# A fused FFT filter and Mish layer: the spectral half rewritten, with a second Mish buffer, DMA copies of the filter and a new instruction order

## The chip, the cores and the metric

The kernel runs on one core of a Trainium2 chip. The metric is the device time of one execution in microseconds, as the median of several executions. A profile covers one execution; its span runs from the first to the last instruction and is 1.3 to 2.1 us shorter than the reported time. PE is the matmul engine, PEld its weight loads, DVE, ACT and POOL are the vector, scalar and GpSimd engines, and SP issues most transfers. No execution here had a second die to compare with, so "slow" only marks runs more than 1.5% above the fastest of the same kernel. The experiments ran on two chips, e5 to e8 and e13 to e15 on one, e1 to e4 and e9 to e12 on the other. The kernel before ran in every round, with medians of 169.0 to 169.6 us.

## The reference, cut to what matters

```python
x = A_x                                   # [1, 2048, 512] bf16
g = sigmoid((x * gate_w).sum(-1))
a = irfft2(rfft2(x) * (w_r + 1j * w_i))   # filter in the frequency domain, fp32
h = x @ w1 + b1                           # 512 -> 1792
b = (h * tanh(softplus(h))) @ w2          # Mish, then 1792 -> 512
return g * a + (1 - g) * b
```

The two dense layers need 448 matmuls of 128 x 128 weights by 512 columns. The FFT is done by matmuls with constant matrices, between which data has to change its layout.

Of the kernel before, what the change touches and what calls it, by code (L numbers as in the profile page):

```python
# [8 lines left out]
BF = mybir.dt.bfloat16  # L9
# [7 lines left out]
NCH = 4  # L17

# [8 lines left out]
def _q_of(c, e):  # L27
    return 64 * c + e


def _build_consts():
    cs = {}
    d = np.arange(D, dtype=np.float64)[:, None]
    k = np.arange(256, dtype=np.float64)[None, :]
    ang = 2 * np.pi * d * k / D
    FD = np.zeros((D, 512))
    FD[:, :256] = np.cos(ang)
    FD[:, 256:] = -np.sin(ang)
    FD[:, 256] = (-1.0) ** np.arange(D)
    cs["FD"] = FD.reshape(4, 128, 512).transpose(1, 0, 2)  # L40
    n = np.arange(D, dtype=np.float64)[None, :]
    kk = np.arange(256, dtype=np.float64)[:, None]
    ang2 = 2 * np.pi * kk * n / D
    GD = np.zeros((512, D))
    GD[:256, :] = 2 * np.cos(ang2)
    GD[256:, :] = -2 * np.sin(ang2)
    GD[0, :] = 1.0
    GD[256, :] = (-1.0) ** np.arange(D)
    GD /= (S * D)
    cs["GD"] = GD.reshape(2, 2, 128, D).transpose(2, 1, 0, 3).reshape(128, 4, D)  # L50
    a = np.arange(64, dtype=np.float64)[:, None]
    e = np.arange(64, dtype=np.float64)[None, :]
    qre = np.array([_q_of(0, ee) for ee in range(64)])
    qim = np.array([_q_of(1, ee) for ee in range(64)])
    M1 = np.zeros((128, 32, 128))
    G1 = np.zeros((128, 32, 128))
    for b in range(32):
        th = -2 * np.pi * e * (32 * a + b) / S
        c_, s_ = np.cos(th), np.sin(th)
        M1[0:64, b, qre] = c_  # L60
        M1[64:128, b, qre] = -s_
        M1[0:64, b, qim] = s_
        M1[64:128, b, qim] = c_
        thi = (2 * np.pi * e * (32 * a + b) / S).T
        ci, si = np.cos(thi), np.sin(thi)
        G1[qre, b, 0:64] = ci
        G1[qim, b, 0:64] = -si
        G1[qre, b, 64:128] = si
        G1[qim, b, 64:128] = ci
    cs["M1"] = M1  # L70
    cs["G1"] = G1
    RF = np.zeros((128, 128))
    RI1 = np.zeros((128, 128))
    for b in range(32):
        for dd in range(32):
            ph = -2 * np.pi * b * dd / 32
            fw = [[np.cos(ph), np.sin(ph)], [-np.sin(ph), np.cos(ph)]]
            iv = [[np.cos(ph), -np.sin(ph)], [np.sin(ph), np.cos(ph)]]
            for m2 in range(2):
                for ci_ in range(2):  # L80
                    for co in range(2):
                        RF[4 * b + 2 * ci_ + m2, 4 * dd + 2 * m2 + co] = fw[ci_][co]
                        RI1[4 * dd + 2 * m2 + co, 4 * b + 2 * ci_ + m2] = iv[co][ci_]
    RI2 = RI1[np.arange(128) ^ 1, :]
    P1k = np.zeros((128, 128))
    P0k = np.zeros((128, 128))
    Jm = np.zeros((128, 128))
    for dd in range(32):
        for m2 in range(2):
            for co in range(2):  # L90
                po = 4 * dd + 2 * m2 + co
                P1k[4 * (31 - dd) + 2 * (1 - m2) + co, po] = 1
                if m2 == 1:
                    P0k[4 * (31 - dd) + 2 + co, po] = 1
                else:
                    P0k[4 * ((32 - dd) % 32) + co, po] = 1
                Jm[po ^ 1, po] = 1
    small = np.stack([RF, RI1, RI2, P0k, P1k, Jm], axis=1)
    cs["SMALL"] = small
    cs["SGN"] = np.where(np.arange(128) % 2 == 0, 1.0, -1.0).astype(np.float32).reshape(128, 1)  # L100
    return cs


class _Task:
    __slots__ = ("name", "eng", "dur", "fn", "deps", "lat", "sem", "semval", "idx", "sig",
                 "start", "done", "succ", "bl", "prio", "xfer", "ninst", "opts", "isdma")

    def __init__(self, name, eng, dur, fn, lat=0.0, prio=0.0):
        self.name = name
        self.eng = eng  # L110
        self.dur = dur
        self.fn = fn
        self.deps = []
        self.lat = lat
        self.sem = None
        self.semval = 0
        self.idx = -1
        self.sig = 0
        self.start = 0.0
        self.done = 0.0  # L120
        self.succ = []
        self.bl = 0.0
        self.prio = prio
        self.xfer = 0.0
        self.ninst = 0
        self.opts = None
        self.isdma = False


OPT_BIAS = {"act": 0.0}  # L130
SCH = dict(eps=0.1, sync=0.1)


class _Cnt:
    def __init__(self, e):
        self._e = e
        self.n = 0

    def __getattr__(self, k):
        f = getattr(self._e, k)  # L140

        def w(*a, **kw):
            self.n += 1
            return f(*a, **kw)  # L144

        return w


class _Graph:
    ENGS = ("pe", "act", "dve", "pool", "sp")  # L150

    def __init__(self):
        self.tasks = []
        self.last_w = {}
        self.readers = {}
        self.cur_prio = 0.0
        self.win_first = None
        self.win_last = None

    def add(self, name, eng, dur, fn, reads=(), writes=(), lat=0.0, deps=(), prio=None):  # L160
        if prio is None:
            prio = self.cur_prio
        t = _Task(name, eng, dur, fn, lat, prio)
        dset = []
        seen = set()

        def _add(d):
            if d is not None and d is not t and id(d) not in seen:
                seen.add(id(d))
                dset.append(d)  # L170

        for d in deps:
            _add(d)
        for r in reads:
            _add(self.last_w.get(r))
        for w in writes:
            _add(self.last_w.get(w))
            for rd in self.readers.get(w, ()):
                _add(rd)
        for r in reads:  # L180
            self.readers.setdefault(r, []).append(t)
        for w in writes:
            self.readers[w] = []
            self.last_w[w] = t
        t.deps = dset
        t.idx = len(self.tasks)
        self.tasks.append(t)
        return t

    def add_multi(self, name, opts, reads=(), writes=(), deps=(), prio=None):  # L190
        e0, d0, f0 = opts[0]
        t = self.add(name, e0, min(o[1] for o in opts), f0, reads=reads, writes=writes, deps=deps, prio=prio)
        t.opts = list(opts)
        return t

    def schedule(self):
        tasks = self.tasks
        for t in tasks:
            t.succ = []
            t.start = -1.0  # L200
        for t in tasks:
            for d in t.deps:
                d.succ.append(t)
        for t in reversed(tasks):
            m = 0.0
            for s_ in t.succ:
                if s_.bl > m:
                    m = s_.bl
            t.bl = t.dur + t.lat + m
        nleft = {id(t): len(t.deps) for t in tasks}  # L210
        ready = [t for t in tasks if not t.deps]
        free = {e: 0.0 for e in self.ENGS}
        order = {e: [] for e in self.ENGS}
        nsched = 0
        EPS = SCH['eps']
        SYNC_LAT = SCH['sync']
        dq_free = 0.0
        dq2_free = 0.0
        while nsched < len(tasks):
            best = None  # L220
            best_est = None
            ests = []
            for t in ready:
                if t.opts is None:
                    est = free[t.eng]
                    for d in t.deps:
                        dd = d.done + (0.0 if d.eng == t.eng else SYNC_LAT)
                        if dd > est:
                            est = dd
                else:  # L230
                    bo = None
                    for (oe, od, of) in t.opts:
                        e_ = free[oe]
                        for d in t.deps:
                            dd = d.done + (0.0 if d.eng == oe else SYNC_LAT)
                            if dd > e_:
                                e_ = dd
                        sc = e_ + od + (OPT_BIAS.get(oe, 0.0) if (self.win_first is not None and self.win_first.start >= 0 and self.win_last.start < 0) else 0.0)
                        if bo is None or sc < bo[0] - 1e-9:
                            bo = (sc, e_, oe, od, of)  # L240
                    est = bo[1]
                    t.eng, t.dur, t.fn = bo[2], bo[3], bo[4]
# [717 lines left out]
```

## The kernel before: what the change and the argument touch

Work is a graph of tasks, each with an engine and an estimated duration; a list scheduler at build time turns it into one instruction order for each engine, with semaphore waits between engines. Every instruction is issued from one helper, so the old profile has one line number (L144) for nearly everything, and one reads it by tile names: `xT` is x transposed, `hsreg` the first layer's output, `ureg` the Mish factor, `bs` the output, `scr` DRAM scratch.

```python
# width FFT: 16 matmuls of 64 x 256 for each of 16 row tiles
ins = e.matmul(ps[64*c:64*c+64, bank, 256*bx:256*(bx+1)], xT[:, dt_, t, bx:128:2],
               FD_sb[:, dt_, 256*c:256*(c+1)], start=(dt_ == 0), stop=(dt_ == 3))
...  # second step, DRAM round trip 1, third step, filter, its inverse, DRAM round trip 2
# inverse width FFT: 4 matmuls of 512 columns for each row tile
ins = e.matmul(ps[:, ybank, :], TT[:, ts_, jj, :], GD_sb[:, jj, :], start=(jj == 0), stop=(jj == 3))
...
# Mish of chunk c, two halves of 3584: exp, ln(1 + .), tanh on ACT in one of two buffers,
# then h * tanh(.) on POOL
G.add(f"{nm}_{c}_{hi}", "act", ..., f_act, ...)
G.add(f"mul_{c}_{fh}_{tl}", "pool", ..., f_mul, ...)
```

## Time and profile before

| | before |
|---|---|
| median time | 169.17 us (169.09 to 169.73) |
| span of the profiled run | 167.8 us |
| PE / DVE / ACT / POOL busy | 156.2 / 100.6 / 118.1 / 78.0 us |
| bytes moved | 24.0 MB |

A row of a window gives its borders, its length, then for each engine the busy time and the instruction count, then the granted PE clock, the DMA share and GB/s. A row of a group gives count, busy time, mean ns of one, and the idle time ahead of it with what ended it. The prediction shows the lines and reads them: PE is busy 93% of the span, and no other engine is above 70%.

### The profile page before, as it was taken

The numbers are of one execution on the slowest core, as the hardware profiler recorded it, in microseconds if no ns is written. First come the engines' busy times: TensorE is split into PE (matmuls) and PEld (weight loads), VectorE is DVE, ScalarE is ACT, GpSimd is POOL, SyncE is SP. The second block draws the span as 40 slices with busy tenths as digits, with TensorE's granted clock in tenths as the row PEclk, the third lists the DMA queues.
The fourth block names the chain that finished last, engine by engine and source line by source line (L and its number), as shares of the span: only waits on it lengthen the run. The fifth ranks groups of instructions, "written<-read, shape, count | busy, mean of one in ns | idle before, by whom it ended". The sixth has DMA issues, their size and how long they took to land.

```text
span 167.8 us, 2686 instructions
## 1 busy us (share of the span) xinstructions
PE 156.2 (93%) x1047; PEld 78.2 (47%) x1047; DVE 100.6 (60%) x170; ACT 118.1 (70%) x90; POOL 78.0 (46%) x79
## 2 busy tenths in 40 slices
PE   1798999995999999999999999999999999999990
PEld 0676733372665333444444444443455555544440
DVE  1233601537577885975799798887167885351533
ACT  3145568792998999999988999999999971220000
POOL 1000160059602699524999800099950399910000
PEclk9999999999999999999999999999999999999998
DMA  5999279992405859400030303035901112000101
GB/s 175 304 413 389 84 263 431 391 399 89 125 0 174 293 164 334 168 4 2 0 125 0 125 0 125 4 125 178 321 4 62 62 64 96 33 34 31 62 0 62
DMA packets 13857, 23.99 MB, mean 143 GB/s; under 512 B 852, under 2 KB 10324, under 8 KB 13076
## 3 DMA queue, kind: packets, MB, share of 16 engines
q1 hardware_dynamic: 13076, 17.77, 30.2%
q0 software_dynamic: 768, 6.05, 9.0%
q8 instruction: 8, 0.13, 0.3%
q14 instruction: 5, 0.04, 0.1%
HBM read 17.52 MB, written 6.29 MB: 142 GB/s over the span
## 4 chain that ended last, share of the span: by engine, by line
PE 77%; DMA 15%; DVE 4%; issue 1%; SPq 1%; ACT 0%; ACTq 0%
PE ps L144 77%; DMA scr<-T 12%; DMA hsreg<-in_A_x_dram 3%; DVE bs L144 2%; DVE T L144 1%; DVE xT L144 1%; SPq L144 1%; DVE hsreg L144 0%; ACT T L144 0%; ACTq L878 0%; SPq L878 0%
## 5 line engine op out<-in xcount | busy, mean ns | idle before, releaser
L144 POOL TENSOR_TENSOR hsreg<-hsreg,ureg 128x896 bf16<-128x896 bf16 x32 | 59.3, 1880 | 14.5 <-ACT ureg L144 14.5
L144 PE MATMUL ps<-xT,w_sb 128*128 128x512 bf16 x224 | 53.2, 380 | 0.2 <-DVE hsreg L144 0.2
L144 PE MATMUL ps<-w_sb,hsreg 128*128 128x512 bf16 x224 | 51.9, 379 | 0.0
L144 ACT ACTIVATE ureg<-ureg 128x3584 bf16<-128x3584 bf16 x16 | 51.0, 3189 | 0.2
L144 DVE TENSOR_SCALAR hsreg<-ps,b1f 128x512 bf16<-128x512 f32 x37 | 27.6, 749 | 14.6 <-PE ps L144 13.4
L144 PEld LDWEIGHTS ps<-xT,w_sb 128*128 128x128 bf16 x224 | 19.1, 97 | 29.9 <-DVE hsreg L144 8.2
L144 PEld LDWEIGHTS ps<-w_sb,hsreg 128*128 128x128 bf16 x224 | 21.6, 98 | 24.5
L144 ACT ACTIVATE ureg<-hsreg 128x3584 bf16<-128x3584 bf16 x8 | 25.5, 3188 | 0.6 <-ACT ureg L144 0.3
L144 DVE TENSOR_SCALAR bs<-ps,omg 128x512 bf16<-128x512 f32 x15 | 11.2, 749 | 16.7 <-PE ps L144 16.6
L144 PE MATMUL ps<-fdgd,xT 128*64 128x256 bf16 x256 | 18.6, 294 | 1.1 <-DMA fdgd<-c_fd 1.0
L144 DVE CAST T<-ps 128x512 bf16<-128x512 f32 x19 | 12.9, 687 | 8.2 <-PE ps L144 8.1
L144 PEld LDWEIGHTS ps<-fdgd,xT 128*64 128x64 bf16 x256 | 14.0, 117 | 4.1 <-issue 1.7
L144 PE MATMUL ps<-fdgd,TT 128*128 128x512 bf16 x64 | 15.4, 379 | 0.0
L144 ACT ACTIVATE hsreg<-ps,b1f 128x512 bf16<-128x512 f32 x19 | 13.0, 685 | 3.4 <-PE ps L144 3.2
L144 DVE SCALAR_TENSOR_TENSOR bs<-ps,gcol,bs 128x512 bf16<-128x512 f32 x16 | 12.0, 749 | 4.2 <-PE ps L144 3.6
L144 DVE COPY xT<-ps 128x512 bf16<-128x512 bf16 x13 | 5.3, 422 | 14.2 <-PE ps L144 14.2
L144 ACT ACTIVATE Abuf<-ps 128x512 bf16<-128x512 f32 x8 | 4.8, 597 | 11.4 <-PE ps L144 11.4
L144 ACT ACT_TABLE_LOAD x9 | 11.5, 1283 | 0.9 <-PEq L945 0.8
L144 ACT ACTIVATE T<-ps 128x512 bf16<-128x512 f32 x13 | 7.5, 593 | 5.0 <-DMA scr<-T 2.9
L144 DVE TENSOR_TENSOR bs<-ps,WaT 128x512 bf16<-128x512 f32 x16 | 10.3, 682 | 0.3 <-PE ps L144 0.3
L144 DVE TENSOR_TENSOR bs<-ps,WbT 128x512 bf16<-128x512 f32 x16 | 10.2, 680 | 0.0
L144 DVE CAST TT<-ps 128x256 bf16<-128x256 f32 x22 | 8.0, 436 | 3.0 <-PE ps L144 3.0
(58 smaller groups left out, 90.5 us busy)
## 6 DMA issues: line engine op xcount, KB each, us to landing
WaT<-in_A_w_r_dram POOLq DMA_DIRECT2D x1, 2056.0 KB, 8.1
WbT<-in_A_w_i_dram POOLq DMA_DIRECT2D x1, 2056.0 KB, 14.0
scr<-T SPq DMA_DIRECT2D x8, 256.0 KB, 3.9
Abuf<-scr SPq DMA_DIRECT2D x2, 1024.0 KB, 6.1
scr<-T SPq DMA_DIRECT2D x4, 512.0 KB, 2.6
Abuf<-scr SPq DMA_DIRECT2D x4, 512.0 KB, 5.3
out_dram<-bs SPq DMA_DIRECT2D x8, 256.0 KB, 2.0
w_sb<-in_B_w_dram SPq DMA_DIRECT2D x2, 896.0 KB, 12.3
```

Of the source, the lines that this page charges most:

```text
L144: return f(*a, **kw)
```

## The change

The intent is less PE work, by a finer factoring of the FFT, and a better packed order. The few words that came with it name only the last steps: a second Mish buffer "so that the last two chunks share table loads", a DMA copy of the filter, eviction writes without stride, and a new order found by search. The diff itself replaces nearly the whole file. Its core, cut:

```diff
+# fold x before the FFT, on POOL: u = left + right half, v = left - right
+return e.tensor_tensor(out=xu[:, a:b_, uv, :], in0=x_sb[:, a:b_, 0:256], in1=x_sb[:, a:b_, 256:512],
+                       op=ALU.add if uv == 0 else ALU.subtract)
+# stages p, d, t, it: 64 matmuls of 128 columns each
+ins = e.matmul(o, xu[:, t, uv, e_:256:2], RF, start=True, stop=True)
+ins = e.matmul(bank(b, c // 2)[:, o:o + 128], zu[:, c, t, :], FD[:, c, :], start=True, stop=True)
 ...
+# evictions: PSUM read with a stride, SBUF written in order
+evac(f"ed{t}", lambda t=t: rD[:, 512*t:512*t+1024].rearrange("p (r u) -> p r u", u=2),
+     lambda b=b2: pair(b).rearrange("p (u r) -> p r u", u=2), 1024, ...)
 ...
+if ri == 0 and wdma:      # upper rows of the real filter part
+    dma(f"{nm}n{fh}", dstv[64:128, f0:f0+32, :], dstv[0:64, f0:f0+32, :], 1.6, ...)
+ubuf = [uT[:], uT[:], uT[:], rW[:, 0:7168] if u3 else uT[:]]   # second Mish buffer, chunk 3
 ...
+# rows 8 to 15 of x transposed by DMA, one DRAM round trip, half-swaps of the spectrum by DMA
-order = G.schedule()      # list scheduler at build time
+G.place(ORDER)            # 539 tasks in a searched order, engine and PSUM slot named for each
```

A piece is the edge step. Frequencies 0 and 256 of each row share a column and are filtered apart, by four small matmuls, two ACT copies, three small DVE operations (xp1, xp2, ead), four more matmuls and a DVE copy. The order keeps POOL off the SBUF port by a dependency behind every DVE task marked `lock`; xp2 and ead, which read two SBUF operands, are not marked.

## The prediction

> **What bounds the kernel now.** I read the share of each engine, then the 40 slices, then the chain that ended last, and last the windows, to see whether the chain's long DMA step is real.
>
> ```profile
> PE 156.2 (93%) x1047; PEld 78.2 (47%) x1047; DVE 100.6 (60%) x170; ACT 118.1 (70%) x90; POOL 78.0 (46%) x79
> ...
> PE   1798999995999999999999999999999999999990
> ```
>
> TensorE (PE) is busy 156.2 of 167.8 us and is below 0.9 only in the first slices, one slice near 42 us, and the last. DVE has 67 us to spare, ACT 50.
>
> ```profile
> 21.46 19.98 DMA scr<-T
> ...
> 56.65 105.60 PE ps L144 x533
> 162.24 0.02 issue
> 162.27 0.76 DVE bs L144
> ```
>
> ```profile
> 24.00:32.00 8.00, 8.00 (x37) 2.68 (x34) 2.86 (x4) 6.63 (x6) 0.00 (x0) 1.00 1.02 423
> 32.00:40.00 8.00, 7.93 (x120) 5.02 (x118) 3.56 (x7) 5.65 (x7) 4.61 (x7) 1.00 0.85 323
> 40.00:48.00 8.00, 5.71 (x75) 4.04 (x76) 4.56 (x7) 6.42 (x5) 4.70 (x3) 1.00 0.23 69
> ```
>
> The chain blames 20 us on a write to DRAM scratch, but the windows (span, then PE's busy time first) show PE at 8.00 and 7.93 of 8 us during it: the transfer is hidden, and only the 2.3 us missing in 40:48 cost anything. From 56.65 to 162.25 nothing but matmuls stands on the chain. So the kernel is bound by the amount of PE work, and I count that first.
>
> The unit prices come from the timeline. Seven 512-column matmuls run from 70.91 to the next group at 72.42: 0.216 us each. Transposes of 128 columns come 12 in 0.84 us, about 0.056 each once the last one's latency of 0.24 is off. The forward FFT along the width, pairs of 64-column tiles, takes 1.0 us per row tile (10.64 to 11.64). PE work of the old kernel: dense 448 x 0.216 = 96.6; x transposes 64 x 0.056 = 3.6; width FFT 16; second step 32 x 0.109 = 3.5; third 16 x 0.216 = 3.5; its inverse 32 x 0.216 = 6.9; inverse second step 64 x 0.056 = 3.6; inverse width FFT 64 x 0.216 = 13.8; gate 1.7. Sum 149. The other 19 us are the wait for x and a half-speed clock at first, the gap at 40, and a tail of 5.6 us after the last matmul (162.2 to 167.8: four DVE operations of 0.75 and an output transfer of about 2).
>
> **What the Trainium skill says.** TensorE: Matmul & The Clock Gate, section "Wait — 56ns, not 53.3ns?", gives 215.7 ns and 55.6 ns for 512 and 128 columns at full clock; the trace agrees with both. ScalarE: Activation LUTs, section "What ACT_TABLE_LOAD costs", gives 1283 ns per load, and the trace shows exactly that (fourth row below; the others, with the mean ns of one after the busy us, are the prices I use):
>
> ```profile
> L144 POOL TENSOR_TENSOR hsreg<-hsreg,ureg 128x896 bf16<-128x896 bf16 x32 | 59.3, 1880 | 14.5 <-ACT ureg L144 14.5
> ...
> L144 ACT ACTIVATE ureg<-ureg 128x3584 bf16<-128x3584 bf16 x16 | 51.0, 3189 | 0.2
> ...
> L144 DVE CAST T<-ps 128x512 bf16<-128x512 f32 x19 | 12.9, 687 | 8.2 <-PE ps L144 8.1
> ...
> L144 ACT ACT_TABLE_LOAD x9 | 11.5, 1283 | 0.9 <-PEq L945 0.8
> L144 ACT ACTIVATE T<-ps 128x512 bf16<-128x512 f32 x13 | 7.5, 593 | 5.0 <-DMA scr<-T 2.9
> ```
>
> VectorE: DVE Perf Modes, section "The perf-mode tier table", puts a bf16 SBUF tensor_tensor of 2048 at 1224 ns. No run here shows it yet (the old DVE multiplies nothing that lies wholly in SBUF); with the author's fixed 0.14 us that leaves 0.53 ns an element, so I estimate 0.68 us for 1024 and 0.55 for 768. SBUF — State Buffer, section "Who interferes with whom", says that a DVE operation with two SBUF inputs and a POOL operation that reads SBUF shut each other out. The old trace can't show that; the new kernel runs many such pairs and orders them itself.
>
> **The change part by part.** The few words name its last steps, but the diff rewrites the whole spectral half. What stays: the two dense layers and Mish, and the PE's 96.6 us.
>
> PE, new: 8 of 16 row tiles are transposed on PE, the others by DMA: 32 x 0.056 = 1.8. The four small transform stages (p, d, t, it) have 64 matmuls of 128 columns each: 256 x 0.056 = 14.3. The inverse to the width (id) 64 x 0.109 = 7.0; the last (ip) 16 x 0.216 = 3.5, of which chunk 3 accumulates straight into the dense output. Gate 1.7, edge and gate rows 0.8. Sum 125.7, **23.5 us less than before**. Thirteen warm-up matmuls (some 2.8 us) lie in the wait for x.
>
> DVE, new, read off the list that names each task's engine. A 1024-element eviction from PSUM I estimate at 687 + 512 x 1.04 = 1.22 us. First dense layer 26 x 1.22 = 31.7; transform evictions 31 x 1.22 = 37.8; filter 22 x 0.68 = 15.0; Mish multiply 23, mixed sizes, 14.2; output scaling 13, 9.5; output adds 8 x 0.42 and one of 0.75, 4.1; input copies 4 x 0.42 = 1.7; filter layout 7 x 0.71, 2 x 1.25 and small ones, 8; gate and edge 3. Sum **about 125, up from 101**. The pieces at 0.71 and 1.25 are the author's figures; nothing in the old trace has them.
>
> ACT, new: Mish has the same elements, but exp in four pieces: per chunk 3 x 7168 x 0.833 ns + 8 x 0.2 = 19.5, so 78.1. Table loads: the list still runs exp2, ln2, tanh2, exp3, ln3, tanh3, so **the second buffer does not bring exp2 and exp3 or ln2 and ln3 together**: nine loads again, 11.5. Nine evictions of 1.02, first layer 2.7, output 2.7, final scaling 11 x 0.67, small 3.5. Sum about 115 against 118.
>
> POOL: 10 pre-additions (18), 9 filter moves (18), 9 multiplies (19), the rest 8: about 64, down from 78. One DRAM round trip in place of two; the upper-row copy by DMA takes two DVE operations of 1.25 us off DVE. Stride-free eviction writes change no duration that I can read here, so I give them nothing.
>
> **Sum on the path.** Start: the old 128 KB piece of x landed at 3.0 us, 1 MB in all by 6.9. The new kernel wants 512 KB of x and 512 KB of w1 first, so I put its first dense matmul at 7.0 us. From there PE has 125.7 - 0.9 = 124.8 us: 131.8. Tail: one half-tile scaling of 0.4 and an output transfer of about 2.1: 134.3 without any wait on the way.
>
> The other two engines give nearly the same floor. ACT: the first exp needs four first-layer tiles, each 0.86, and some transform work on PE, and two evictions: about 14 us. From the first exp to the last tanh the list puts 78.1 + 8 x 1.28 + 16.2 of other ACT work = 104.5: last tanh ends at 118.5. Behind the start of that tanh (2.7 long) PE still has 16.9 us listed, so 118.5 - 2.7 + 16.9 + 2.5 = 135. DVE: 125 between 6 and the end: 131 plus 2.1. **Three engines with floors within 2 us of each other** can't all be fed without gaps. I add 4% of 125 = 5 us for waits between them: **139.5 us**.
>
> **Rivals.** (1) PE work alone sets it, as before. For: the old PE lost only 2.3 us in mid-kernel. Against: it had 50 and 67 us of slack on ACT and DVE. That gives 134 to 136. (2) DVE becomes the bound, because two-input operations and POOL block each other, or because the estimated forms are slower than assumed. For: 125 of 139 us, and each 2% of it is 2.5 us. Against: DVE's PSUM reads, over half of its work, have no second SBUF input. That gives 143 to 148. (3) The DRAM round trip starves PE: 256-byte rows written, then read into rows freed only when filter moves are done. For: the old trace lost 2.3 us behind the same thing at 512-byte rows. Against: between the last write and its first user the list puts 13.6 us of PE work, which a write of 3.9 and a read of 6.1 us (the old medians) fit into. It would cost 2 to 4 us: 141 to 144. (4) Nothing gained, since ACT sets the end. Against: the ACT chain, counted whole, ends at 118. I see no way to 166.
>
> **Range and chances.** The floor is 134, and my sum would have to be 15% off to reach 160. Eight times in ten: 134.5 to 147. Faster by over 2%: 0.97; within 2%: 0.02; slower: 0.01.
>
> **What would show each step.** PE work: matmul count 448 of 512 columns, and far fewer of the rest; about 23 us less busy time. DVE: at 85% or more of the span. ACT: nine table loads, exp and ln alternating by chunk. Waits: PE windows of the middle 2 to 5% below full, its wait behind DVE evictions rather than DMA; if a gap of several us stands before the t stage with a scratch transfer named, rival 3 is right. Start: first dense matmul at 7 us. Tail: 2.5 us behind the last matmul. The prediction is wrong if the early loads or the DMA transposes are late, if DVE's SBUF forms are slower than estimated, or if the waits between three full engines cost 10 us rather than 5.

## The result, and the profile after

The changed kernel took 145.27 us (144.63 to 145.88, four runs), against 169.13 for the kernel before; six more runs later gave 145.32 (143.21 to 145.92), of which the three at 145.9 count as slow, since one run was at 143.21. The ratio of the fast runs was 0.8715 (0.862 to 0.8809) at first and 0.8575 (0.8498 to 0.8651) in the repeat. Ratios are the mean time of one kernel's fast runs over that of the other's of the same rounds, so not quite the ratio of the medians, which is 0.859 at first. The gain is 24 us of 169, where 29.7 were predicted.

The page of the kernel after, with the busy shares and the slices of PE and of the PE clock:

```profile
PE 132.6 (93%) x921; PEld 73.2 (51%) x921; DVE 119.4 (84%) x154; ACT 112.8 (79%) x77; POOL 63.3 (44%) x50
...
PE   4789999889969999999999999997799999999992
...
PEclk9969999999999999999999999999999999999999
```

PE's busy time fell by 23.6 us, from 156.2 to 132.6; the work count of the prediction said 23.5. That they agree to 0.1 is partly luck: the 132.6 holds 2.9 us of warm-up that the count leaves out, and in both kernels PE was busy some 7 us longer than counted (156.2 against 149, 132.6 against 125.7). DVE rose to 119 (125 predicted), ACT is at 113 (115) and POOL at 63 (64). So the engine loads are nearly right, and the miss must lie mostly in starts, clock, gaps and ends. The slices show three dips: the PE clock at 0.6 in the third slice, PE at 6 near 40 us, and PE at 7 near 98.

The chain that ended last, in order of time (start, length, what), shows two of them:

```profile
0.80 4.62 DMA rA<-in_A_x_dram
...
7.70 3.35 PE ps L897 x8
...
12.14 4.32 PE ps L897 x20
...
96.43 0.14 PE ps L801
...
96.60 0.28 ACT tmp L809
...
96.90 0.28 ACT tmp L810
...
97.24 1.19 issue
98.43 0.16 DVE ezb L745
98.59 0.20 DVE tmp L811
...
98.82 1.91 DVE tmp L813
```

The first eight dense matmuls take 3.35 us, 0.42 each; the twenty at 12.14 take 0.216 each. So the array ran at half clock there. Two windows show when:

```profile
4.56:7.98 3.42, 1.86 (x19) 1.07 (x19) 0.85 (x2) 1.19 (x2) 2.33 (x3) 1.00 1.02 353
7.98:11.39 3.41, 3.41 (x12) 1.28 (x10) 0.00 (x0) 0.00 (x0) 3.24 (x2) 0.50 1.09 382
```

The transposes of x just before had run at full speed (8 in 0.62 us from 5.47). So here the clock had been released and was lost again, after 3.4 us in which PE was busy 1.86 us and never idle for longer than 0.74 at a time. And from 96.4 to 102.9 the chain leaves PE for the edge step. The timeline there (start, length, engine, line, operation):

```profile
96.24 6.11 POOL L933 TENSOR_TENSOR rD<-rD,uT 128x1024 bf16<-128x1024 bf16 x3 [3.14 <-ACT uT L921]
...
97.20 1.30 DVE L812 TENSOR_TENSOR tmp<-tmp,wsi 128x128 f32<-128x128 f32 x1 [0.87 <-ACT tmp L810]
...
98.82 1.91 DVE L813 TENSOR_TENSOR tmp<-tmp 128x128 bf16<-128x128 f32 x1
...
100.78 0.20 PE L820 MATMUL ps<-tmp,rD 128*128 128x1 bf16 x2 [1.63 <-DVE tmp L813]
...
102.55 3.85 ACT L918 ACTIVATE rW<-hs 128x2048 bf16<-128x2048 bf16 x2 [2.01 <-DVE hs L904]
```

xp2 (L812) and ead (L813) work on 128 elements a partition, yet take 1.30 and 1.91 us, while POOL multiplies from 96.24 to 102.35. PE loses 1.63 us behind ead. ACT loses 2.01 behind an eviction that stands after them on DVE.

The rows that answer to the prices of before, from the groups by form:

```profile
L514 DVE CAST rD<-ps 128x1024 bf16<-128x1024 f32 x7 | 8.4, 1214 | 0.0
...
L776 DVE TENSOR_TENSOR rC<-rC,rW 128x1024 bf16<-128x1024 bf16 x8 | 5.5, 687 | 0.2 <-DMA tmp<-rC 0.2
...
L920 ACT ACT_TABLE_LOAD x4 | 5.1, 1283 | 0.1
```

The estimates of 1.22 us for an eviction and 0.68 for a filter multiply hold. Table loads are four here, three on L921 and one each on L517 and L743, nine as before.

### The profile page after: what moved, and what is told of

Read it like the earlier page. It is cut to its first block, busy times and chain, and to the rows that moved or that the text cites. A ratio compares the mean times of both kernels' runs of the same rounds, so it can differ in the third digit from the quotient of the medians.

```text
span 142.7 us, 2358 instructions
## 1 busy us (share of the span) xinstructions
PE 132.6 (93%) x921; PEld 73.2 (51%) x921; DVE 119.4 (84%) x154; ACT 112.8 (79%) x77; POOL 63.3 (44%) x50
## 4 chain that ended last, share of the span: by engine, by line
PE 78%; ACT 11%; DVE 4%; DMA 3%; issue 2%
PE ps L949 33%; PE ps L897 27%; PE ps L876 5%; ACT uT L920 4%; DMA rA<-in_A_x_dram 3%; PE ps L837 3%; PE ps L762 3%; ACT uT L921 3%; PE ps L975 2%; PE ps L637 2%; PE ps L603 2%; PE ps L649 1%; DVE tmp L813 1%; ACT L921 1%; ACT L920 1%
## 5 line engine op out<-in xcount | busy, mean ns | idle before, releaser
L897 PE MATMUL ps<-rX,w_sb 128*128 128x512 bf16 x224 | 53.0, 387 | 0.9 <-DVE rX L514 0.5
L949 PE MATMUL ps<-w_sb,hs 128*128 128x512 bf16 (+1 forms) x182 | 40.0, 363 | 0.0
L897 PEld LDWEIGHTS ps<-rX,w_sb 128*128 128x128 bf16 x224 | 21.4, 99 | 26.0 <-issue 1.6
L949 PEld LDWEIGHTS ps<-w_sb,hs 128*128 128x128 bf16 x182 | 17.5, 98 | 17.4 <-DVE hs L933 0.3
L904 DVE TENSOR_TENSOR hs<-ps,b1f 128x1024 bf16<-128x1024 f32 x19 | 23.2, 1227 | 0.9 <-PE ps L897 0.6
L920 ACT ACTIVATE uT<-uT 128x4096 bf16<-128x4096 bf16 (+1 forms) x6 | 19.1, 3190 | 0.1
L921 ACT ACTIVATE uT<-uT 128x4096 bf16<-128x4096 bf16 (+1 forms) x6 | 19.1, 3186 | 0.1
L618 POOL TENSOR_TENSOR rB<-rA 128x1024 bf16<-128x1024 bf16 (+1 forms) x10 | 17.3, 1735 | 4.1 <-DMA rA<-in_A_x_dram 3.2
L918 ACT ACTIVATE uT<-hs 128x2048 bf16<-128x2048 bf16 (+1 forms) x8 | 13.6, 1694 | 5.5 <-DVE hs L904 5.3
L933 POOL TENSOR_TENSOR rD<-rD,uT 128x1024 bf16<-128x1024 bf16 (+1 forms) x7 | 13.4, 1918 | 6.8 <-DVE rD L933 3.2
L949 PE MATMUL ps<-w_sb,rD 128*128 128x512 bf16 x56 | 13.2, 379 | 0.0
L517 ACT ACTIVATE rC<-ps 128x1024 bf16<-128x1024 f32 x8 | 8.0, 1018 | 0.2
```

The costliest lines, as they stand in the source:

```text
L517: return e.activation(o(), i(), AF.Copy)
L618: return e.tensor_tensor(out=xu[:, a:b_, uv, :], in0=x_sb[:, a:b_, 0:256], in1=x_sb[:, a:b_, 256:512], op=ALU.add if uv == 0 else ALU.subt ...
L897: ins = e.matmul(bank(b, i), w1_sb[:, dt_, 128 * ft:128 * (ft + 1)], xT[:, c, dt_, :, :], start=(dt_ == 0), stop=(dt_ == 3))
L904: return e.tensor_tensor(out=hs[hb][:, ft:ft + 2, :], in0=pair(b).rearrange("p (f s) -> p f s", f=2), in1=b1f[:, ft:ft + 2].unsqueeze(2).t ...
L918: return e.activation(o, hsf[hb][:, 512 * a:512 * b_], fn_)
L920: return e.activation(o, o, fn_, bias=1.0)
```

## The experiments

**Theory:** PE's work is still the bound, and the miss is a cold start of the PE clock, the edge step behind POOL, and the difference of span and reported time (how far that held is said below, in the section on the prediction). **Rivals:** DVE, now loaded for 84% of the span, is the bound; or the ACT chain of Mish is. Each kernel below differs from the changed kernel, or from the one named as base, only as shown, and gives the reference's result unless said otherwise.

**e1: more warm-up matmuls.** The warm-up's memset goes first on POOL, and there are 20 matmuls, so that PE is busy until x lands.

```diff
-ones cRF x0 ident warm0 w1_0 ...
+warm0 cRF x0 ones ident w1_0 ...
-NWARM = 13
+NWARM = 20
```

> The first eight dense matmuls took 0.42 us each (half clock) because the 13 warm-up matmuls ended at 4.7 us and x came at 5.4. Here the warm-up starts 0.6 us earlier and has 20 matmuls, so PE is busy until x lands. Theory (PE work and its order set the start of the chain): those eight matmuls take 0.22 us each, first exp starts 1.6 us earlier, total 1.0 to 1.8 us shorter. Rival (the middle is bound by DVE or ACT, which absorb it): clock full, but total within 0.4 us.

Measured: 143.15 us (142.76 to 143.53), 2.1 less. The timeline of PE:

```profile
1.17 3.92 PE L537 MATMUL ps<-hs 128*128 128x256 bf16 x20 [1.17 <-POOL hs L526]
...
7.74 1.90 PE L897 MATMUL ps<-rX,w_sb 128*128 128x512 bf16 x8 [0.52 <-DVE rX L514]
```

The same eight matmuls need 1.90 us in place of 3.35, from the same start, and the first exp of chunk 3 begins at 101.37 in place of 102.55. The spread shrank too. The Trainium skill (TensorE: Matmul & The Clock Gate, section "What's actually happening") says that about 3.4 us of sustained work release the clock, in a window that runs free of the kernel; the old warm-up of 13 lasted 2.9 us. The runs agree in part. With 13, the profiled runs of e2 and e3 below reached the dense matmuls at full clock, that of e9 ran even its transposes at half speed (16 in 2.33 us), and the one above had the clock and lost it. So a short warm-up can fail in two ways; e1, which makes it both longer and nearly gapless up to x, does not tell them apart. The ten runs of the changed kernel lie at 143.2 us (one), 144.6 to 144.8 (four) and 145.8 to 145.9 (five), which fits these three starts, but only two of the ten were profiled.

**e2: the edge step freed from POOL.** One POOL multiply goes to DVE, which was idle 0.87 us there, and POOL may start the next only behind ead.

```diff
-... es0::1 mul2_0_0:pool es1 ...
+... es0::1 mul2_0_0:dve es1 ...
-G.add("ead", "dve", ..., writes=[ey_])
+G.add("ead", "dve", ..., writes=[ey_], lock=True)
```

> In the edge step two small DVE operations on SBUF (xp2, ead; some 0.28 us each) took 1.30 and 1.91 us while POOL multiplied. Here the first of these POOL multiplies goes to DVE, ahead of them, and POOL starts only after ead. Theory (the shared port makes DVE wait for POOL's whole instruction): xp2 and ead about 0.3 us each, the PE gap of 1.6 us near 99 and the ACT gap of 2.0 near 101 mostly close, total 1.0 to 2.5 us shorter. Rival (they are slow because they are fp32 or because of start partitions): they keep 1.3 and 1.9 us and the total stays within 0.5 us.

Measured: four fast runs at 141.0 to 142.6 us, two slow ones at 143.3 and 144.0 (cold starts, as e5 and e13 suggest, but these two were not profiled); median of all 141.9, of the fast ones 141.2. The timeline of DVE and ACT:

```profile
95.59 0.29 DVE L812 TENSOR_TENSOR tmp<-tmp,wsi 128x128 f32<-128x128 f32 x1 [0.24 <-ACT tmp L810]
...
96.18 0.29 DVE L813 TENSOR_TENSOR tmp<-tmp 128x128 bf16<-128x128 f32 x1
```

```profile
96.17 2.75 ACT L921 ACTIVATE uT<-uT 128x3072 bf16<-128x3072 bf16 x1
98.82 5.84 ACT L918 ACTIVATE rW<-hs 128x2048 bf16<-128x2048 bf16 x3
```

Both operations fall to 0.29 us with the same operands and types, so the time was spent waiting for POOL and not on fp32. ACT goes from tanh of chunk 2 into exp of chunk 3 without its gap of 2 us. This is the exclusion that the prediction quoted from SBUF — State Buffer; the runs agree, and show that DVE waits for the end of the POOL instruction. In the changed kernel ead starts at 98.82 and ends at 100.72, and POOL's multiply runs from 98.43 to 100.57. xp1, with one operand in PSUM and one in SBUF, took its usual 0.28 us at 98.50, inside the same multiply.

**e3: one eviction moved from ACT to DVE.** PE stops 1.13 us near 40.5 behind the eviction ep12, which waits on ACT behind a tanh of 3.6 us.

```diff
-wrm010:dve ... wim000:dve ... wrm000:dve ... ep12:act wim101:dve mul0_0_3:dve ... mul0_0_1:dve
+ep12:dve ... wrm010:dve ... wim000:dve ... mul0_0_3:dve ... wrm000:dve mul0_0_1:dve wim101:dve
```

> The eviction ep12 sits in ACT's queue behind tanh of chunk 0, and PE stops 1.1 us at 40.5 until it is done. Here it is on DVE, ahead of four filter moves of 0.7. Theory (in-order ACT queue holds PE): the gap at 40 goes away, total 0.5 to 1.3 us shorter if PE is on the path there. Rival (DVE is the bound in this stretch, and 1.2 us more of it costs as much as is gained): within 0.5 us.

> The three edits together. Theory (three gaps on one chain, each cost its own time): total shorter by nearly the sum of the three, 2.5 to 5 us, so about 141 us. Rival (one engine's total is the bound): the sum is not reached, less than the largest single gain plus 0.5 us.

Measured: e3 took 146.18 us (144.28 to 147.43, two of six slow), no gain; its fastest run is 1.1 us above the fastest of the changed kernel (143.21). e4, the three edits together, took 142.36 (141.88 to 142.69), where e5 below, the same without this eviction, took 141.13. In e4 PE gained at 40 and lost more later: against e5 it is busy 16.56 in place of 15.93 us from 24 to 42, but 22.17 in place of 23.80 from 42 to 66. The sum was not reached; the 1.2 us on DVE came back as waits for DVE (1.9 us for first-layer evictions, 0.4 in e5). Here the rival of a full DVE is right, and the loss is even larger than it said.

**e5: warm-up and edge together.**

> Twenty warm-up matmuls and the edge step freed from POOL, without the moved eviction of e3. The edge edit alone ran at 141.0 to 144.0 us, in two groups 2.5 us apart, the warm-up edit alone within 0.8. Theory (the two groups are cold and warm starts, and the edge gap is worth 2 us or more): all runs within 0.8 us of each other, median 140.6 to 141.4, so the faster group of the edge edit every time. Rival (the groups have another cause): still spread over 2 us or more, median 142 or more.

Measured: 141.13 us, five runs from 140.97 to 141.37 and one, unexplained, at 142.31. It beats both kernels, 169 and 145.3. Its window after the edge step, and the one before, show PE full:

```profile
66.00:94.00 28.00, 28.00 (x182) 14.32 (x179) 25.78 (x39) 27.17 (x19) 7.41 (x4) 1.00 0.67 152
94.00:104.00 10.00, 10.00 (x78) 5.73 (x77) 9.30 (x15) 9.38 (x8) 5.47 (x4) 1.00 0.00 0
```

**e6 to e8: which engine is the bound?** All on the base of e1 (143.15 us). e6 replaces ln by exp, so that the table never changes, and e7 filters an eighth of the columns; both give a wrong result. e8 repeats 14 matmuls.

```diff
-(("exp", AF.Exp, EXPP), ("ln", AF.Ln, HALF), ("tanh", AF.Tanh, HALF))    # e6
+(("exp", AF.Exp, EXPP), ("ln", AF.Exp, HALF), ("tanh", AF.Tanh, HALF))
-out=Y[:, fa:fb, :], in0=Y[:, fa:fb, :], in1=Wr[:, fa:fb, 0:128]          # e7, and so for p2 and ad
+out=Y[:, fa:fa + 1, :], in0=Y[:, fa:fa + 1, :], in1=Wr[:, fa:fa + 1, 0:128]
+if c == 2 and ft == 9:                                                   # e8
+    for _ in range(14):
+        e.matmul(bank(b, i), w1_sb[:, 0, 0:128], xT[:, c, 0, :, :], start=True, stop=True)
```

> Wrong result on purpose: ln is replaced by a second exp of the same size, so that no table has to be changed between; eight loads of 1.28 us, 10.3 us of ACT work, are gone, more than any sharing between two chunks could save. On the base of the 20 warm-ups (143.15 us). Theory (PE and DVE carry nearly as much as ACT, so ACT's time is not the bound alone): 1 to 4 us shorter. Rival (the ACT chain from the first exp to the last tanh sets the end): 7 to 10 us shorter.

> Wrong result on purpose: the filter multiplies and adds only an eighth of its columns, which takes some 12 us off DVE between 74 and 96 us (and 4 off POOL). On the base of the 20 warm-ups (143.15 us). Theory (there PE is busy 22.00 of 22 us and DVE is not the bound): at most 2 us shorter, by a smaller stop before chunk 3. Rival (DVE is the bound of the whole): 6 us or more shorter.

> Fourteen more matmuls of 512 columns (3.0 us of PE, same result) in the first layer of chunk 2, near 60 us, where PE has no gap. On the base of the 20 warm-ups (143.15 us). Theory (PE is on the path from 42 to 96 us): 2.5 to 3.2 us longer. Rival (DVE or ACT is the bound, PE has room): under 1 us longer.

Measured: e6 142.08 us (141.96 to 142.47), 1.1 less for 10 us less ACT (102.8 busy); e7 143.49 (143.17 to 143.80), no gain for 10 us less DVE (109.7); e8 146.10 (145.61 to 146.41), 2.95 more for 3.0 us more PE. e7's page and its window of the stretch show it:

```profile
PE 132.5 (94%) x928; PEld 73.7 (52%) x928; DVE 109.7 (78%) x154; ACT 112.8 (80%) x77; POOL 60.0 (43%) x50
```

```profile
66.00:94.00 28.00, 28.00 (x181) 14.27 (x179) 15.91 (x38) 27.17 (x19) 3.95 (x4) 1.00 0.67 147
```

DVE is busy 15.9 of 28 us in place of 25.6 in e1, and PE is full in both. In e6 the wait of 1.1 us for ep12 near 40 is gone, which is as much as the gain. So PE is the bound from 42 us on, but for the edge step, and both rivals fall there. This holds for the doses tried: e12 below adds 2.5 us of DVE work near 50 us, and there DVE becomes the bound. e6 also caps what any sharing of table loads could bring: about 1 us for all eight.

**e9: the changed kernel again.**

> The changed kernel itself, unchanged, to have it on the chip and in the rounds of the others. Theory (its start is cold in some executions and warm in others): 144 to 146.5 us with a spread of over 1 us, where every kernel with 20 warm-up matmuls stayed within 1.4. Rival (the spread of the first four runs was chance): all within 0.5 us of 145.3.

Measured: 143.21, 144.69, 144.76, 145.88, 145.91 and 145.92 us. The profiled run, at 145.88, has a cold start again, of the other kind: the transposes are slow too, and the first eight dense matmuls take 3.60 us from 8.24. Its trace has no record of the clock, and the windows then show 1.00 throughout; the spacing of the matmuls (0.43 us) is the safer sign of a cold start. The spread is 2.7 us, against 0.8 in e1.

**e10 to e12: the named parts, one by one undone**, on the base of e1.

```diff
-rD[...].rearrange("p (r u) -> p r u", u=2), pair(b).rearrange("p (u r) -> p r u", u=2)   # e10, ed and ey
+rD[...].rearrange("p (r u) -> p u r", u=2), pair(b).rearrange("p (u r) -> p u r", u=2)
-u3=1, wdma=1     # e11: one Mish buffer; mul2_0_1, mul2_0_2, mul2_1_1 moved ahead, to DVE
+u3=0, wdma=1
-u3=1, wdma=1     # e12: the copy on DVE
+u3=1, wdma=0
```

> The 16 evictions ed and ey go back to reading PSUM in order and writing every second element of SBUF (same result), on the base of the 20 warm-ups (143.15 us). Theory (an eviction is paced by its PSUM read of one fp32 an element, so the write's stride costs nothing): one eviction stays at 1.22 us, total within 0.5 us. Rival (the strided 2-byte write costs, which is why the change took it out): 1.5 us or more for one eviction, total 1 us or more longer.

> One Mish buffer for all chunks again: exp of chunk 3 must wait for the multiplies of chunk 2, of which three are moved ahead and to DVE so that the order is possible. On the base of the 20 warm-ups (143.15 us). Theory (the second buffer lets exp of chunk 3 start while the multiplies of chunk 2 still read; PE has other work meanwhile): first exp of chunk 3 later by 1 to 3 us, total 0.5 to 3 us longer, nine table loads in both. Rival (the buffer saves table loads): one or two more table loads without it.

> The copy of the filter's real part to the upper rows goes back from two DMAs to two DVE operations of some 1.2 us, near 46 us, on the base of the 20 warm-ups (143.15 us). Theory (PE is the bound, DVE has little room there, at 5.8 of 6 us): 0.5 to 2 us longer. Rival (DVE has room or PE does not wait for it): within 0.4 us.

Measured, e10: 143.27 us (143.21 to 143.69), 0.1 more. One eviction takes 1.30 us in place of 1.22, more than the theory's nothing and less than the rival's 1.5, and it is hidden.

e11: 145.39 us (144.96 to 145.61), 2.2 more, with nine table loads. Exp of chunk 3 starts at 102.80, against 101.37 in e1, and stops again after two pieces, for the multiplies of chunk 2. So the second buffer does help, by letting chunk 3 start, and not by table loads. The moved multiplies are part of this number.

e12: 147.41 us (145.94 to 147.91), 4.3 more for two DVE operations of 1.24, over twice what I expected. The waits of PE and the windows:

```profile
PE ps L897 <- DVE rD L904: 2.8, 1, 2.8
```

```profile
58.00:62.00 4.00, 1.24 (x5) 0.60 (x6) 3.79 (x6) 3.97 (x3) 1.60 (x6) 0.93 0.77 262
62.00:66.00 4.00, 4.00 (x14) 1.50 (x12) 2.85 (x3) 3.97 (x2) 0.80 (x1) 0.65 0.94 315
```

The chain that ended last lies on DVE from 44.58 to 60.71. The later DVE makes PE wait 2.8 us, and after that wait the granted clock is 0.65 from 62 to 66; weight loads of dense matmuls follow each other every 0.43 us there (61.83, 62.26, 62.69), where 0.216 is usual. Five of the six runs have a mean clock of 0.987 or 0.988 and took 147.1 to 147.9; the one with 0.999 took 145.94, so the lost clock may be worth some 1.5 us of the 4.3, as far as one run shows. A filter move of 0.70 us, now at 52.4 us, took 1.93 there, while POOL was busy 1.81 of 2 us. It has one SBUF input; that it, too, waited for POOL fits the times but was not tested.

**e13 to e15: the cold start measured, and DVE early and in the middle**, on the base of e5 (141.13 us). e14 and e15 cut three first-layer evictions into 8 pieces each.

```diff
-NWARM = 20     # e13
+NWARM = 1
+if c == 1 and ft in (8, 2, 4):     # e14; e15: c == 2 and ft in (4, 6, 10)
+    for k in range(8): ...         # 64 of 512 columns, two tiles
```

> The best version so far (20 warm-up matmuls and the edge step freed from POOL, 141.13 us) with one warm-up matmul in place of 20, so that the start is cold in every execution. Theory (the cold start costs its 1.6 to 2 us at the end too): 142.7 to 144 us. Rival (later waits absorb it): within 0.5 us of 141.13.

> Three first-layer evictions of chunk 1, between 29 and 38 us, cut into 8 pieces each (same result), which adds an estimated 2 to 4 us of DVE work; on the best version so far (141.13 us). Theory (PE is the bound of the whole, but in the first third it waits behind DVE): total longer by most of what the three evictions grow by. Rival (DVE has room there too): under a third of it.

> The same with three first-layer evictions of chunk 2, near 60 us, where PE has no gap; on the best version so far (141.13 us). Theory: total longer by under half of what the evictions grow by, less than in the early dose. Rival (DVE is the bound everywhere): longer by as much as in the early dose.

Measured: e13 143.84 us (143.62 to 144.29), 2.7 more in every run, with the eight matmuls at 3.48 us from 8.55. So the cold start is not absorbed later. The dose was smaller than I expected: 24 pieces are busy 5.0 us (e14) and 4.8 (e15) in place of 3.7, so 1.3 and 1.1 more. e14 took 141.73 us (141.61 to 142.31), 0.6 more, about half of it and so between theory and rival; e15 took 141.04 (140.79 to 141.37), nothing. In the first third PE does wait behind DVE at times, in the middle DVE has room for one more us.

## Why the prediction came out as it did

The direction and the mechanism were right: the gain is the PE work removed, and PE remains the bound (e8). The other loads were within 6 us, the nine table loads came as said, and the stride of the writes hardly changes the total. The predicted time was 5.8 us too low. The median of 145.27 lies inside the stated range of 134.5 to 147, but the ratio of the first rounds, 0.8715, lies just above its upper end (147 of 169.17, or 0.869).

In the prediction's own terms, the profiled run of the changed kernel compares like this:

| | predicted | measured |
|---|---|---|
| first dense matmul | 7.0 us | 7.7 us |
| PE work from there | 124.8 us | 128.3 us |
| stops of PE | 5 us | 4.0 us |
| behind the last matmul | 2.5 us | 2.7 us |
| sum, the span | 139.3 us (stated as 139.5) | 142.7 us |
| reported time | taken as the same | 144.63 us |

So the steps that failed are the start and the clock, and the step from span to time. The waits were right in size and wrong in cause:

- **"I put its first dense matmul at 7.0 us. From there PE has 125.7 - 0.9 = 124.8 us."** It began at 7.70, and the 124.8 priced every matmul at full clock. The warm-up was booked as lying in the wait for x, without asking whether the clock is at full when x has come. The cold start cost 1.6 us in the profiled run (PE stops behind ep12 at 40.50, against 38.84 in e2, which began its dense matmuls at the same 7.70 and at full clock), 2.1 by e1's median, and 2.7 where it happens every time (e13). Of the 3.5 us of extra PE work this explains about half. The rest, 1.5 us, is there in e5 too, and no run takes it apart.
- **The sum ended at the end of the span and was given as the reported time.** The profiled span was 142.7 us and its time 144.63. That is 1.9 us; the old kernel's 167.8 and 169.17 would have shown 1.4.
- **"I add 4% of 125 = 5 us for waits between them."** PE stopped for 4.0 us after its first dense matmul, 1.63 of it behind ead and 1.13 behind ep12, and not at all from 67 to 96 us, where DVE is busy 92% and ACT 97% of the time. Floors within 2 us of each other did not make three bounds; 10 us off ACT or off DVE gained 1.1 us and nothing. The exclusion of DVE and POOL was named, but as a rival that slows DVE as a whole, and "gate and edge 3" priced the edge by DVE's time. It fell on two operations of a serial step. Removing that gave 2.0 us (e5 against e1), so the edge took part of the 5 us and does not explain why the sum was too low.

That e5's span, 139.3 us, equals the predicted sum is luck: its dense matmuls begin at 8.07, PE works 126.3 us from there, stops for 2.3 and leaves a tail of 2.7.

Of the rivals, the first was nearest in mechanism. By its number, 143 to 148 us, the second holds the result, but DVE is not the bound (e7). The third, a starved round trip, does not show: PE lost 0.16 us ahead of stage t. The fourth fell with the gain of 24 us.

## What to carry to other kernels

Count the work of the bounding engine first, but price the start at the clock that it will really have, keep the array busy from the first instruction until data comes, and don't mix span and reported time. A short serial step that leaves the bounding engine deserves its own look: two DVE operations of 0.29 us cost 2 us because POOL held the port, and moving one multiply from POOL to DVE, with one more dependency, gave it back. When an order is searched with a cost model, look for what the model doesn't know, here the port and the clock.

## What the Trainium skill lacked or had wrong

- TensorE: Matmul & The Clock Gate, section "What's actually happening": it puts the fall to half clock after at least one idle window of about 3.4 us. In e12 a PE wait of 2.8 us was followed by half clock, 0.65 on average from 62 to 66 us. In the changed kernel's profiled run the clock fell at 7.98 after 3.4 us in which PE was busy 1.86 us and idle for at most 0.74 at a time, so no wholly idle window was needed.
- The same page, section "Back-to-back issue gap", gives about 131 ns for sustained 512-column matmuls in a real kernel and calls 216 an over-count. Here they ran at 0.216 us at full clock: 20 in 4.32 us.
- ScalarE: Activation LUTs, section "What ACT_TABLE_LOAD costs", adds a drain of about 1.38 us to each load. Here exp ended at 28.01, the load ran 28.03 to 29.31, and ln started at 29.32: a switch cost 1.3 us.
- None of the pages named here has a time for an eviction that writes every second bf16 element of SBUF: 1.30 us against 1.22 for 1024 fp32 elements a partition (e10, where PSUM is then read in order, so the two sides are changed together).
